# Fused attention and feed-forward kernel: copies of the turned output from another queue, and a second matmul in four 32-column tiles in chosen sessions

## The chip, the cores and the metric

The kernel runs on one core of a Trainium2 chip. The metric is the device time of one execution in microseconds; lower is better. A core has five engines that run side by side: PE (TensorE: matmuls, with weight loads listed apart as PEld), DVE (VectorE), ACT (ScalarE), POOL (GpSimd) and SP (SyncE, which here only issues transfers). Each engine executes its own instructions in the order in which they stand.

## The reference, cut to what matters

Two layers in a row. The first is attention through 32 inducing points: `h = mab(I, x)`, then `mab(x, h)`, for B = 4 batches of N = 12480 tokens with C = 128 channels. The second is a feed-forward layer with a leaky activation on each of the 49920 tokens.

```python
def mab(q, kv):                      # scale = 1/sqrt(128)
    s = scale * (q @ kv.transpose(0, 2, 1))
    s = s - s.max(-1, keepdims=True)
    a = np.exp(s)
    a /= a.sum(-1, keepdims=True) + 1e-09
    return a @ kv
h = mab(I, x)                        # I: (4, 32, 128), x: (4, 12480, 128)
y = mab(x, h)                        # (4, 12480, 128)
u = y @ w_in                         # w_in: (128, 2048)
g = np.maximum(u, 0.0) + alpha * np.minimum(u, 0.0)
out = g @ w_out                      # w_out: (2048, 128), float32
```

## The kernel before, in words

A batch is cut into six "supers" of 2048 tokens and a rest of 192. A super has four groups of 512 tokens, so a batch has NG = 25 groups (24 full ones and the rest), numbered g. The hidden width 2048 is cut into 16 blocks of 128: four row bands r times four steps j. The main loop goes over sessions (b, g, j), four to a group, two to the rest group.

What a session does, in the order of the code (lines 829 to 836):

- `fill` (line 433): four matmuls `ring<-rep,hW`, one per band r. Each contracts only 32 rows (the 32 attention weights, replicated into four partition bands in `rep`) with `hW = h @ w_in`, and writes 128 hidden units x 512 tokens to a bank of PSUM. Six banks form a ring. Then four ReLUs `gt<-ring`, some on ACT (line 457) and some on DVE (line 459); which go where is written out ahead of time by `make_plan` (line 756), a beam search over assumed costs in ns. In `make_plan` every task has a cost tuple (PE ns, engine, engine ns).
- the tasks set for the session (`at(slot, fn, j, cost)`, line 708, slot = 25 b + g). For the current batch: `b_scores` (attention scores of the next super; 128 rows contracted, four outputs of 32 partitions each), `b_rep`, `b_den`. For the next batch: `a_load` (x by a GpSimd transfer, line 131), `a_xpose` (transfer that transposes x into `xT`, issued by SP, line 145), `a_scores` (`ring<-xT,IT`, 32-partition outputs), `a_accum` (pooling, `ring<-xn,e1T`, 16 matmuls with 32-partition outputs), `h_weights` (the next batch's hW) and some small ones.
- `move(2)` (line 833): takes two entries from the list `moves`, see below.
- `mm2` of the session before (line 463): four matmuls `acc<-gt,W`, with the 128 x 128 block of the scaled `w_out` as weights and 512 tokens streaming, adding up to `acc` in PSUM, output channels on the partitions.

The output of a group therefore stands turned (channels by tokens). When a group is complete, `finish` (called by `flush` in the next session's `fill`) calls `turn` (line 537): DVE transposes 32 x 32 squares into `yT` (line 541), and after the fourth group of a super 16 `shuffle` transfers and one `leave` are put on `moves`. A shuffle (line 550) copies 32 partitions x 2 KB of `yT` to another band of 32 partitions in `yq`, SBUF to SBUF, 64 KB. `leave` (line 554) has POOL multiply by the reciprocal denominators (four instructions, line 559) and issue the 1 MB store (line 569). `yT`, `yq` and `obw` have two buffers each. The last super of the last batch and the rest groups are not turned: there `gt` is the weight operand, and `ob` (two buffers) is stored directly (lines 526 and 535).

`pin` keeps every engine's instructions, transfers included, in program order: a transfer that waits holds up what stands behind it on the same queue. The transfers of SP land in one hardware queue (q1 in the profile), those of GpSimd in a software queue (q0); the 16 DMA engines serve both.

Of the kernel before, what the change touches and what calls it, by code (L numbers as in the profile page):

```python
# [24 lines left out]
def kernel(  # L25
# [30 lines left out]
    def pin(bi):  # L56
        ins = bi.ins
        e = ins.engine
        if e in last:
            tc.add_manual_dep(  # L60
                ins,
                last[e],
                mybir.DependencyInfo(
                    mybir.DependencyClass.NoSync, mybir.DependencyReason.DATA
                ),
                reason="program order",
            )
        last[e] = ins.name
        return bi
# [26 lines left out]
    def mm(o, lhsT, rhs, start=True, stop=True, **kw):  # L96
        return pin(nc.tensor.matmul(o, lhsT, rhs, start=start, stop=stop, **kw))  # L97
# [160 lines left out]
    def a_scores(st, u):  # L258
        ps = bank()
        if u < NS:  # L260
            for q in range(NQ):
                mm(ps[32 * q : 32 * q + 32, :], IT[:], st.xT[:, u, q, :])
            e1 = work.tile([P, GRP], bf16, name="e1", tag="e1")
            pin(nc.scalar.activation(  # L264
                out=e1[:], in_=ps[:], func=EXP, scale=scale, accum_out=st.es[:, u : u + 1]
            ))
            e1T = work.tile([P, NB, P], bf16, name="e1T", tag="e1T")
            pin(nc.sync.dma_start_transpose(out=e1T[:], in_=e1[:]))
        else:
            mm(ps[0:M, :REM], IT[:], st.xTr[:].rearrange("c j p -> c (j p)"))  # L270
            pin(nc.scalar.activation(
                out=e1r[:, :, :PR],
                in_=ps[0:M, :REM].rearrange("m (j p) -> m j p", j=JR),
                func=EXP, scale=scale, accum_out=st.es[0:M, u : u + 1],
            ))
            e1T = work.tile([P, JR, M], bf16, name="e1Tr", tag="e1Tr")
            pin(nc.sync.dma_start_transpose(
                out=e1T[:], in_=e1r[:].rearrange("m j p -> m (j p)")
            ))
        st.e1T[u] = e1T  # L280
# [69 lines left out]
    def b_scores(st, s):  # L350
        ps = bank()
        if s < NS:
            for q in range(NQ):
                mm(ps[32 * q : 32 * q + 32, :], st.hT, st.xT[:, s, q, :])
            e2 = work.tile([P, GRP], bf16, name="e2", tag="e2")
            pin(nc.scalar.activation(out=e2[:], in_=ps[:], func=EXP, scale=scale_of(st)))  # L356
            w = GRP
        else:
            mm(ps[0:M, :REM], st.hT, st.xTr[:].rearrange("c j p -> c (j p)"))
            e2 = work.tile([M, REM], bf16, name="e2r", tag="e2r")  # L360
            pin(nc.scalar.activation(out=e2[:], in_=ps[0:M, :REM], func=EXP, scale=scale_of(st, M)))
            w = REM

        nq = NQ if s < NS else 1
        st.d[s] = dram.tile([32 * nq, w], bf16, name="e2d", tag="e2d" if s < NS else "e2dr")
        pin(nc.sync.dma_start(out=st.d[s][:], in_=e2[:]))
        st.e2[s] = e2
# [45 lines left out]
    def turned(b, g):  # L413
        return g < NS * NQ and (b, g // NQ) != (B - 1, NS - 1)
# [10 lines left out]
    def move(n):  # L425
        for _ in range(min(n, len(moves))):
            moves.pop(0)()
# [32 lines left out]
        flush()  # L460
        return gt

    def mm2(st, g, j, gt):
        pp, nb, cp = shape_of(g)
        acc = acc_of(st.b, g)
        begun = (g % 2 == 1 and st.b + g > 1) or cp > 1
        for r in range(4):
            if turned(st.b, g):
                mm(
                    flat(acc), W1[:, r * NJ + j, :], gt[:, r, :],  # L470
                    start=(j == 0 and r == 0 and not begun),
                    stop=False, skip_group_check=True,
                )
                continue
            for i in range(cp):
                c = r * NJ + j * cp + i
                for k in range(nb):
                    k0 = (i * nb + k) * pp
                    mm(
                        acc[:pp, k, :], gt[:, r, k0 : k0 + pp], W1[:, c, :],  # L480
                        start=(j == 0 and r == 0 and i == 0 and k == 0 and not begun),
                        stop=False, skip_group_check=True,
                    )
        if j == NJ // cp - 1 and st.b * NG + g > 0:
            held.append((st, g))
# [51 lines left out]
    def turn(st, s, q, acc):  # L537
        if q == 0:
            st.yT[s] = wide_pool.tile([P, 4, NQ, NB, 32], f32, name="yT", tag="yT")
        yT = st.yT[s]  # L540
        pin(nc.vector.transpose(  # L541
            out=yT[:, :, q, :, :].rearrange("p a j c -> p j a c"),
            in_=acc[:].rearrange("p j (a c) -> p j a c", a=4),
        ))
        if q < NQ - 1:
            return
        yq = wide_pool.tile([P, 4, NQ, NB, 32], f32, name="yq", tag="yq")

        def shuffle(a, k):
            pin(nc.sync.dma_start(  # L550
                out=yq[32 * a : 32 * a + 32, k], in_=yT[32 * k : 32 * k + 32, a]
            ))

        def leave():
            rd = st.rden[s]
            ob = wide_pool.tile([P, NQ, NB, C], f32, name="obw", tag="obw")
            for q in range(NQ):
                rq = rd[:, :, q : q + 1]
                pin(nc.gpsimd.tensor_tensor(  # L559
                    out=ob[:, q].rearrange("p j (k c) -> p j k c", k=4),  # L560
                    in0=yq[:, :, q].rearrange("p k j c -> p j k c"),
                    in1=bass.AP(
                        tensor=rq.tensor, offset=rq.offset,
                        ap=[rq.ap[0], rq.ap[1], [0, 4], [0, 32]],
                    ),
                    op=MULT,
                ))
            t0 = st.b * N + s * SUP
            pin(nc.gpsimd.dma_start(  # L569
                out=out[t0 : t0 + SUP, :].rearrange("(p q) c -> p (q c)", p=P),  # L570
                in_=ob[:].rearrange("p q j c -> p (q j c)"),
            ))

        for a in range(4):
            for k in range(4):
                moves.append(lambda a=a, k=k: shuffle(a, k))
        moves.append(leave)
# [125 lines left out]
             for j in range(NJ // shape_of(g)[2])]  # L703
    states = {0: st}
    tasks = {}


    def at(slot, fn, j=1, cost=None):
        tasks.setdefault((slot, j), []).append((fn, cost))

    def late_finish():
        linear(st, [0])
# [9 lines left out]
    for b in range(B):  # L722
        base = b * NG
        for s in range(1, NS + 1):
            g = base + s * NQ - 4
            at(g, lambda b=b, s=s: b_scores(states[b], s), 3, (320, "A", 490))
            at(g + 1, lambda b=b, s=s: b_rep(states[b], s), 3)
            at(g + 2, lambda b=b, s=s: b_den(states[b], s), 3, (130, "D", 250))
        if b + 1 < B:
            n = b + 1  # L730

            def begin(n=n):
                states[n] = new_batch(n)

            at(base, begin)
            for i, u in enumerate(order):
                k = base + i * (NG - 13) // NS
                at(k, lambda n=n, u=u: a_load(states[n], u))
                at(k + 3, lambda n=n, u=u: a_xpose(states[n], u))
                at(k + 5, lambda n=n, u=u: a_scores(states[n], u), 0, (320, "A", 680))  # L740
                at(k + 8, lambda n=n, u=u: a_accum(states[n], u), 3, (240, "D", 220))
            k = base + NG - 5
            at(k, lambda n=n: h_sum(states[n]))
            at(k, lambda n=n: h_den(states[n]), 3, (250, "D", 500))
            at(k + 1, lambda n=n: h_transpose(states[n]), 1, (300, "D", 250))
            at(k + 1, lambda n=n: h_weights(states[n]), 3, (320, "D", 600))
            at(k + 2, lambda n=n: b_scores(states[n], 0), 1, (320, "A", 490))
            at(k + 2, lambda n=n: h_linear(states[n]), 3, (80, "D", 250))
            at(k + 3, lambda n=n: b_rep(states[n], 0), 0)
            at(k + 3, lambda n=n: b_den(states[n], 0), 1, (130, "D", 250))  # L750
# [78 lines left out]
    for b, g, j in fills:  # L829
        gt = fill(states[b], g, j)  # L830
        for fn, _ in tasks.pop((b * NG + g, j), []):
            fn()
        move(2)
        if prev is not None:
            mm2(*prev)
        prev = (states[b], g, j, gt)
    mm2(*prev)
    move(len(moves))
# [32 lines left out]
```

The softmax here doesn't subtract the row's maximum and nothing guards it: scores larger than these inputs give would overflow.

## Time and profile before

| | before |
|---|---|
| median of 8 runs (lowest to highest) | 603.64 us (599.92 to 617.72) |
| the profiled execution, its own time | 603.91 us |
| its span on the core | 602.1 us |
| PE busy | 573.7 us (95%), 4518 matmuls |
| DVE busy | 517.9 us (86%) |
| ACT busy | 502.3 us (83%) |
| POOL busy | 143.7 us (24%) |
| main loop, first to last matmul | from 24.9 us to 593.4 us |
| mean granted clock of PE | 0.984 |

Busy times overlap, so they do not add up to the span. The page names shapes as weights (rows * columns), then what streams: "128\*32 128x512" is a matmul that contracts 128 rows into 32 outputs while 512 columns stream. In the timeline the first column is the start in microseconds, the second the length of the merged stretch; in brackets stand the idle time before it and what ended it. [...]the distance between starts, not the length, is what it costs in a row of others.

### The profile page before, as it was taken

To read this page: it belongs to the slowest core of one execution; us is meant where nothing else is said; L and a number is where in the kernel's file an instruction comes from. 1 tells how busy PE (TensorE), PEld (TensorE's weight loads), DVE (VectorE), ACT (ScalarE), POOL (GpSimd) and SP (SyncE) were. 2 spreads that over 40 slices of the span, in tenths; PEclk is the share of its full clock that TensorE was granted. 3 is DMA by queue.
4 is the path that set the end of the run, shared out by engine and by line. 5 is a ranking of instruction groups with operands and counts; after the bars stand their busy time and mean duration, and the time that the engine had idled before them with its cause. 6 is when DMAs were issued, how large, how long until landed. Compare 5 with 4: busy or idle time off the path is not lost.

```text
span 602.1 us, 12844 instructions
## 1 busy us (share of the span) xinstructions
PE 573.7 (95%) x4518; PEld 209.6 (35%) x4518; DVE 517.9 (86%) x869; ACT 502.3 (83%) x987; POOL 143.7 (24%) x196
## 2 busy tenths in 40 slices
PE   5899997999999998999999999799999999999994
PEld 4533332333343332333333333233334333333373
DVE  3588996889989997998988899698998999999983
ACT  2579886888889986888889999689888999999983
POOL 6620123032034030302330403203113303203303
PEclk9899998999999999999999999899999999999998
DMA  9794587973558859777346978797445443353343
GB/s 198 180 191 80 127 187 154 206 205 84 153 161 205 176 152 194 174 162 205 119 120 158 210 171 187 150 210 186 106 144 158 147 105 111 85 175 123 106 141 117
DMA packets 95216, 93.66 MB, mean 156 GB/s; under 512 B 60224, under 2 KB 75856, under 8 KB 92208
## 3 DMA queue, kind: packets, MB, share of 16 engines
q1 hardware_dynamic: 86288, 53.03, 39.1%
q0 software_dynamic: 8720, 39.29, 24.2%
q8 instruction: 35, 0.57, 0.4%
q10 hardware_dynamic: 144, 0.52, 0.2%
q14 instruction: 29, 0.24, 0.1%
HBM read 40.20 MB, written 28.75 MB: 115 GB/s over the span
## 4 chain that ended last, share of the span: by engine, by line
PE 81%; DMA 9%; SPq 4%; issue 2%; ACT 2%; DVE 1%; POOL 1%; POOLq 0%; DVEq 0%; ACTq 0%
PE acc L97 56%; PE ring L97 23%; DMA xT<-xn 6%; SPq L550 2%; ACT gt L457 2%; PE ring L174 1%; SPq L374 1%; DMA winT<-w_in_b 1%; DMA ind_f<-in_inducing_dram 1%; DMA out_dram<-ob 1%; POOL obw L559 1%; SPq L145 1%; DMA rep<-e2d 0%; DVE xT L180 0%; DMA e2d<-e 0%
## 5 line engine op out<-in xcount | busy, mean ns | idle before, releaser
L457 ACT ACTIVATE gt<-ring 128x512 bf16<-128x512 f32 x899 | 469.7, 599 | 67.2 <-PE ring L97 32.6
L459 DVE TENSOR_SCALAR gt<-ring 128x512 bf16<-128x512 f32 x669 | 434.0, 685 | 58.1 <-PE ring L97 51.0
L97 PE MATMUL acc<-gt,W 128*128 128x512 bf16 x1472 | 385.8, 385 | 0.3 <-DVE yT L541 0.3
L559 POOL TENSOR_TENSOR obw<-yq,rd 128x512 f32<-128x512 f32 x92 | 93.3, 1038 | 406.4 <-DMA yq<-yT 284.4
L97 PEld LDWEIGHTS <-W 128*128 128x128 bf16 x1472 | 115.4, 98 | 165.9 <-issue 78.0
L97 PE MATMUL ring<-rep,hW 32*128 32x512 bf16 (+1 forms) x1600 | 159.5, 382 | 0.7 <-DVE hW L250 0.2
L97 PEld LDWEIGHTS <-hW 32*128 32x128 bf16 x1600 | 41.4, 91 | 162.9 <-issue 158.6
L541 DVE STREAM_TRANSPOSE yT<-acc 128x512 f32<-128x512 f32 x92 | 65.0, 706 | 1.9 <-PE acc L97 1.9
L97 PE MATMUL acc<-W,gt 128*128 128x128 bf16 (+1 forms) x384 | 25.6, 220 | 0.0
L97 PEld LDWEIGHTS <-gt 128*128 128x128 bf16 (+1 forms) x384 | 21.9, 106 | 4.2 <-issue 3.8
L97 PE MATMUL acc<-rep,hA 32*128 32x512 bf16 x92 | 17.6, 374 | 0.0
L264 ACT ACTIVATE e<-ring 128x512 bf16<-128x512 f32 x18 | 10.9, 604 | 6.7 <-PE ring L97 6.7
L97 PE MATMUL ring<-xT,IT 128*32 128x512 bf16 x72 | 7.2, 389 | 9.5 <-DMA xT<-xn 9.5
L131 POOL DMA_DIRECT2D xn<-in_x_dram x28 | 15.4, 555 | 2.4 <-DMA xn<-in_x_dram 1.6
L569 POOL DMA_DIRECT2D out_dram<-obw x23 | 13.7, 596 | 6.8 <-POOL obw L559 6.8
L199 ACT ACTIVATE e1t<-ring 128x256 bf16<-128x256 f32 (+1 forms) x13 | 4.8, 371 | 10.8 <-PE ring L97 10.6
L180 DVE COPY xT<-ring 128x1024 bf16<-128x1024 bf16 (+1 forms) x12 | 8.0, 670 | 5.2 <-PE ring L174 4.8
L356 ACT ACTIVATE e<-ring 128x512 bf16<-128x512 f32 x18 | 11.0, 612 | 0.0
L97 PE MATMUL ring<-xT,hT 128*32 128x512 bf16 (+1 forms) x98 | 10.6, 391 | 0.0
L535 POOL DMA_DIRECT2D out_dram<-ob x7 | 3.8, 537 | 27.2 <-DVE ob L526 27.0
L174 PE MATMUL ring<-ident,xn 128*128 128x128 bf16 x96 | 8.8, 249 | 0.9 <-DVE xn L672 0.9
L97 PEld LDWEIGHTS <-hT 128*32 128x32 bf16 (+1 forms) x122 | 3.7, 93 | 11.9 <-issue 11.8
(91 smaller groups left out, 135.2 us busy)
## 6 DMA issues: line engine op xcount, KB each, us to landing
yq<-yT SPq DMA_DIRECT2D x368, 64.0 KB, 2.3
out_dram<-obw POOLq DMA_DIRECT2D x23, 1024.0 KB, 4.9
rep<-e2d SPq DMA_DIRECT2D x92, 128.0 KB, 2.8
xn<-in_x_dram POOLq DMA_DIRECT2D x18, 512.0 KB, 8.8
e2d<-e SPq DMA_DIRECT2D x24, 128.0 KB, 3.9
xn<-in_x_dram POOLq DMA_DIRECT2D x10, 256.0 KB, 8.6
w_out_f<-in_moe_w_out_dram POOLq DMA_DIRECT2D x4, 256.0 KB, 11.1
out_dram<-ob POOLq DMA_DIRECT2D x4, 256.0 KB, 3.8
```

Of the source, the lines that this page charges most:

```text
L97: return pin(nc.tensor.matmul(o, lhsT, rhs, start=start, stop=stop, **kw))
L131: pin(nc.gpsimd.dma_start(out=xn[:, i * w : (i + 1) * w, :], in_=src[:, i * w : (i + 1) * w, :]))
L174: pin(nc.tensor.transpose(tp[:, k * P : (k + 1) * P], xn[:, q, j * C : (j + 1) * C], ident[:]))
L180: pin(nc.vector.tensor_copy(out=dst, in_=tp[:, :w]))
L264: pin(nc.scalar.activation(out=e1[:], in_=ps[:], func=EXP, scale=scale, accum_out=st.es[:, u : u + 1]))
L356: pin(nc.scalar.activation(out=e2[:], in_=ps[:], func=EXP, scale=scale_of(st)))
L457: pin(nc.scalar.activation(out=gt[:, r, :w], in_=ps[:, :w], func=RELU))
L459: pin(nc.vector.tensor_relu(gt[:, r, :w], ps[:, :w]))
L541: pin(nc.vector.transpose(out=yT[:, :, q, :, :].rearrange("p a j c -> p j a c"), in_=acc[:].rearrange("p j (a c) -> p j a c", a=4),))
L550: pin(nc.sync.dma_start(out=yq[32 * a : 32 * a + 32, k], in_=yT[32 * k : 32 * k + 32, a]))
L559: pin(nc.gpsimd.tensor_tensor(out=ob[:, q].rearrange("p j (k c) -> p j k c", k=4), in0=yq[:, :, q].rearrange("p k j c -> p j k c"), in1=ba ...
L569: pin(nc.gpsimd.dma_start(out=out[t0 : t0 + SUP, :].rearrange("(p q) c -> p (q c)", p=P), in_=ob[:].rearrange("p q j c -> p (q j c)"),))
```

## The change

It has four parts. `mm2` gets a flag `narrow`: with it, each 128 x 128 weight block is used as four blocks of 32 columns, each with its own matmul over the same 512 streaming tokens and its own 32 output partitions. The flag is set for a session with a score task (`b_scores`, `a_scores`), a pooling task (`a_accum`) or `h_weights`. The shuffles are issued by GpSimd instead of SP. In the last super of the last batch four entries of `moves` are taken per session instead of two. And the PE costs that `make_plan` assumes for the flagged tasks are lower (320 becomes 215, 240 becomes 200).

```diff
-    def mm2(st, g, j, gt):
+    def mm2(st, g, j, gt, narrow=False):
         pp, nb, cp = shape_of(g)
         acc = acc_of(st.b, g)
         begun = (g % 2 == 1 and st.b + g > 1) or cp > 1
         for r in range(4):
+            if turned(st.b, g) and narrow:
+                for i in range(4):
+                    sl = slice(32 * i, 32 * i + 32)
+                    mm(
+                        flat(acc)[sl, :], W1[:, r * NJ + j, sl], gt[:, r, :],
+                        start=(j == 0 and r == 0 and not begun),
+                        stop=False, skip_group_check=True,
+                    )
+                continue
             if turned(st.b, g):
                 mm(
                     flat(acc), W1[:, r * NJ + j, :], gt[:, r, :],
...
         def shuffle(a, k):
-            pin(nc.sync.dma_start(
+            pin(nc.gpsimd.dma_start(
                 out=yq[32 * a : 32 * a + 32, k], in_=yT[32 * k : 32 * k + 32, a]
             ))
...
+    narrows = set()
...
-    def at(slot, fn, j=1, cost=None):
+    def at(slot, fn, j=1, cost=None, narrow=False):
         tasks.setdefault((slot, j), []).append((fn, cost))
+        if narrow:
+            narrows.add((slot, j))
...
-            at(g, lambda b=b, s=s: b_scores(states[b], s), 3, (320, "A", 490))
+            at(g, lambda b=b, s=s: b_scores(states[b], s), 3, (215, "A", 490), narrow=True)
...
-                at(k + 5, lambda n=n, u=u: a_scores(states[n], u), 0, (320, "A", 680))
-                at(k + 8, lambda n=n, u=u: a_accum(states[n], u), 3, (240, "D", 220))
+                at(k + 5, lambda n=n, u=u: a_scores(states[n], u), 0, (215, "A", 680), narrow=True)
+                at(k + 8, lambda n=n, u=u: a_accum(states[n], u), 3, (200, "D", 220), narrow=True)
...
-            at(k + 1, lambda n=n: h_weights(states[n]), 3, (320, "D", 600))
-            at(k + 2, lambda n=n: b_scores(states[n], 0), 1, (320, "A", 490))
+            at(k + 1, lambda n=n: h_weights(states[n]), 3, (215, "D", 600), narrow=True)
+            at(k + 2, lambda n=n: b_scores(states[n], 0), 1, (215, "A", 490), narrow=True)
...
-        move(2)
+        move(4 if b == B - 1 and g >= (NS - 1) * NQ else 2)
         if prev is not None:
-            mm2(*prev)
+            mm2(*prev, narrow=(b * NG + g, j) in narrows)
```

## The prediction

> **What bounds the kernel now.** I read the page first (busy shares, clock, DMA issues), then the timeline of PE through ordinary sessions, then every place where PE departs from that rhythm, with the timelines of SP and POOL beside it, then the tail. First PE in a plain stretch and in two sessions with tasks (start, length).
>
> ```profile
> PE 573.7 (95%) x4518; PEld 209.6 (35%) x4518; DVE 517.9 (86%) x869; ACT 502.3 (83%) x987; POOL 143.7 (24%) x196
> 200.14 0.40 PE L97 MATMUL ring<-rep,hW 32*128 32x512 bf16 x4
> 200.46 0.40 PE L97 MATMUL ring<-xT,IT 128*32 128x512 bf16 x4
> 200.79 1.04 PE L97 MATMUL acc<-gt,W 128*128 128x512 bf16 x4
> 201.76 0.40 PE L97 MATMUL ring<-rep,hW 32*128 32x512 bf16 x4
> ...
> 221.09 0.40 PE L97 MATMUL ring<-xT,hT 128*32 128x512 bf16 x4
> 221.32 0.40 PE L97 MATMUL ring<-xn,e1T 128*32 128x128 bf16 x16
> 221.65 1.04 PE L97 MATMUL acc<-gt,W 128*128 128x512 bf16 x4
> ```
>
> There are no gaps: PE sets the pace, 1.62 us for the score session (200.14 to 201.76) and 1.30 for a plain one. The starts also give the price of a change of tile shape. Scores followed by pooling, both with 32-column tiles, take 0.23 (221.09 to 221.32); scores followed by full-width mm2 take 0.33 (200.46 to 200.79), and fill to mm2 0.33. A change of shape costs 0.10 us.
>
> Now the largest break in that rhythm, with the transfers around it and DMA shares by stretch (the last three columns are granted clock, DMA share, GB/s).
>
> ```profile
> 73.42 4.06 POOL L559 TENSOR_TENSOR obw<-yq,rd 128x512 f32<-128x512 f32 x4 [39.24 <-DVE gt L459]
> 77.78 0.60 POOL L569 DMA_DIRECT2D out_dram<-obw  x1 [0.30 <-POOL obw L559]
> 78.38 1.07 POOL L131 DMA_DIRECT2D xn<-in_x_dram  x2
> ...
> 79.20 2.33 SPq L550 DMA_DIRECT2D yq<-yT  x2
> 84.35 6.63 SPq L145 DMA_TRANSPOSE xT<-xn  x1
> ...
> 90.06 0.40 PE L97 MATMUL ring<-rep,hW 32*128 32x512 bf16 x4
> 93.64 0.40 PE L97 MATMUL ring<-xT,IT 128*32 128x512 bf16 x4 [3.19 <-DMA xT<-xn]
> 99.02 0.40 PE L97 MATMUL ring<-rep,hW 32*128 32x512 bf16 x4
> ...
> 84.00:88.00 4.00, 4.00 (x25) 1.23 (x24) 3.93 (x7) 3.59 (x8) 0.00 (x0) 1.00 1.08 220
> 96.00:100.00 4.00, 4.00 (x19) 1.13 (x18) 2.78 (x5) 2.90 (x7) 0.09 (x1) 0.73 0.58 141
> ```
>
> PE waits 3.19 us for a transposed x, and the granted clock then falls (0.73 in 96 to 100). From 90.06 to 99.02 lie three sessions, worth 1.62 + 1.30 + 1.30 = 4.22; they took 8.96, so 4.74 is lost. The same place in the next two batches: three sessions from the fill at 233.98 to that at 242.22 lose 4.02, three from 377.49 to 386.44 lose 4.73. That is 13.5 in all. The cause: POOL had stood 39 us in its first `leave`, then issued a 1 MB store and two loads of x at once. The transposition of SP stands behind shuffles and meets DMA engines that are full (share 1.08), so it lands after 9.25 us where others take 4.3.
>
> Last, the tail.
>
> ```profile
> 588.28 4.06 POOL L559 TENSOR_TENSOR obw<-yq,rd 128x512 f32<-128x512 f32 x4 [5.50 <-issue]
> 593.38 1.07 POOL L535 DMA_DIRECT2D out_dram<-ob  x2 [0.16 <-issue]
> 598.01 0.42 DVE L526 TENSOR_TENSOR ob<-acc,rdr 96x256 f32<-96x256 f32 x1 [5.76 <-DMA out_dram<-ob]
> ```
>
> PE is done at 593.4; the last multiply starts at 598.0, since its buffer is held by a store that POOL could issue only behind the late `leave`.
>
> **The change part by part.**
>
> *Narrow mm2.* The order of the built program has 944 matmuls of 32 columns in place of 236, so 59 sessions are narrow. Counting changes of shape along PE's order gives 852 before and 799 after: 53 fewer, x 0.104 us = 5.5. Six sessions win nothing, since a full-width task stands between. What the narrow form itself costs: 708 more matmuls and weight loads. Here a rule speaks against the change. The Trainium skill, "TensorE: Matmul & The Clock Gate", section "Part 3: Packing small matmuls", says that weight loads overlap running matmuls only when their row groups differ; all narrow loads use all rows. By its "LDWEIGHTS" formula (columns / 1.2 ns) 16 loads of 32 columns would stand in the open, an estimate of 0.43 us per session, 25 us in all. The row of pooling answers: 16 loads and 16 matmuls of 4 x 128 columns took 0.33 with the change of shape, so 0.23 for 512 streamed columns per tile, the same as four score matmuls in one go. Those 16 loads added nothing, and they had a quarter of the streaming to hide in that narrow mm2 has. I take 0, with ends 0 and +25.
>
> *Evacuation.* ACT and DVE get the same instructions (899 and 669 ReLUs in both orders), in another split. A plain session asks of them 899 x 0.525 + 669 x 0.65 = 907 us over 392 sessions, 1.16 each of two engines, and about 0.09 for the transposes: 1.25 against PE's 1.30. A session with `a_scores` adds 0.75 on ACT: 1.25 + 0.38 = 1.63 against a shortened 1.52. Its neighbours have slack 0.05 each. Cost 0.1 in at most 18 sessions, some of it absorbed: +1.0, range 0 to 3.
>
> *Shuffles on POOL.* All 368 issues leave SP and enter POOL. The nearest rows are POOL's own issues, which show no dependence on size.
>
> ```profile
> L131 POOL DMA_DIRECT2D xn<-in_x_dram x28 | 15.4, 555 | 2.4 <-DMA xn<-in_x_dram 1.6
> L569 POOL DMA_DIRECT2D out_dram<-obw x23 | 13.7, 596 | 6.8 <-POOL obw L559 6.8
> ```
>
> At 0.555 us that is 204 us more on an engine busy 24%. Per super POOL then has 16 x 0.555 = 8.9, last landing 2.0, `leave` 4.4, store 0.6, two loads 1.1: 17.0. Supers come every 21.6 us at the closest (`yT` of the last batch complete at 506.07, 527.76). So POOL keeps up. Its order changes: the first `leave` stands behind 16 shuffles that can start when `yT` is complete (53.6), end at 62.6 and land by 65. So `leave` runs at 65 instead of 73.4, the store goes out at 69; of the loads around it one follows the shuffles at 62.6, one the store at 70, and the next comes behind the second super's shuffles at 85 (`yT` complete at 75.9). In the built order each of these loads has a shuffle batch or a `leave` between it and the next, so the pile of store plus two loads at 78 dissolves. Behind the waiting `leave` stand only loads with more than 10 us to spare. On SP the transposition at 84.35 loses its shuffles: scores at 79.0 let its small predecessor go near 80.5, it follows at 82, and at 4.4 us lands near 86.5, 3 us before PE asks. So the three breaks go: -13.5, and with them two waits of 0.5 for `xT` (260.8, 272.9) and one of 0.6 for `rep` (123.1), which I count at half, -0.8.
>
> A second rule speaks against this part: the skill's "DMA: Bandwidth & Descriptors", section "Issuing engines are not separate DMA queues", says that all issuers end on the same 16 engines and that spreading them saves only the sequencers' issue time. Taken alone, only the 0.59 us issues go from SP, the engines stay full at 84 to 92, and the breaks stay: the 14.3 drop out of the sum. Agreed for the bytes; but what the trace shows as full is a pile made by POOL's order, and the order changes. I take 14.3, range 0 to 15.1.
>
> *Four moves at the end.* The last super's `yT` is complete at 571.0; 16 issues end at 580, `leave` runs 582 to 586 and the store leaves at 586.5, 6 us earlier. The stores behind it land near 592, before the last multiply is due (593.5). Gain 598.0 - 593.6 = 4.4, less 0.5 for the multiply before it: -3.9, range 0 to -4.5. If that cover fails, the late store holds DVE, and the 4.4 stay.
>
> Sum: 602.1 - 5.5 - 13.5 - 0.8 - 3.9 + 1.0 = 579.4 of span, plus 1.8 around it (603.91 - 602.1): 581.2. The profiled execution is 0.27 above the median of 603.64, so 581 us against the median.
>
> **The rivals.**
>
> *The DMA breaks stay* (or move to another load), by the second rule: 581 + 14.3 = 595. For it: shuffles now share one in-order software queue with loads and stores, so a shuffle behind a load lands with it, 8 us later, and POOL waits. Against: the spacing above.
>
> *Evacuation binds.* ACT and DVE are at 83 and 86%; if the shape changes saved on PE turn into waits for banks, the 5.5 return: 581 + 5.5 = 586.5. For it: waits of 0.15 to 0.2 us near the `h` tasks today.
>
> *POOL becomes the bound, slower.* If one shuffle holds POOL longer than the loads do, POOL takes 16 x + 8.1 per super against 21.6; it decides from x = 0.85 us on. At 1.1 us it needs 25.7, 4 us x 23 supers = 94 too much, less the 23 of gains: near 675; at 0.95 us, 23.3, 39 too much: near 620. DVE would stand at `yT`, then ACT and PE behind full banks. Against: POOL's issues stand at 0.53 to 0.60 us in back-to-back rows; but none of them goes SBUF to SBUF over 32 partitions.
>
> *Open weight loads:* 581 + 25 = 606, slower.
>
> That the change does not do what it says is out: the built order shows the 944 narrow matmuls and POOL's 368 issues.
>
> **How the numbers follow.** The main case 0.60, breaks stay 0.14, evacuation binds 0.13, POOL bound 0.07, open loads 0.03, a mixture near the old time 0.03. A measurement of this kernel can tell about 0.5% (3 us) from no change. Faster by more: 0.60 + 0.14 + 0.13 = 0.87; within: 0.03; slower: 0.10. Low end: all breaks and waits (15.1), tail 4.5, shapes 6, no cost: 578, and 1 less for the spread of runs: 577. The high end takes in the evacuation case and most of the stay case: 595. Left out are the slower cases and the edges, 0.2.
>
> **What would show it.** Right: mm2 narrow at 0.97 us from start to fill, 0.23 instead of 0.33 before it; the xT waits and clock dips near 90, 234 and 378 gone; POOL near 345 us busy with issues of 0.56; the last multiply within 1 us of PE's end. Wrong: a shuffle issue over 0.85 us on POOL, DVE waiting before L541, weight loads opening gaps inside narrow mm2, or waits for xT at other loads.

## The result, and the profile after

| | before | after |
|---|---|---|
| median | 603.56 us (32 runs, 599.41 to 617.72) | 597.78 us (11 runs, 586.55 to 608.72) |
| profiled execution, its span | 602.1 us | 585.0 us (its time 586.80) |
| PE busy | 573.7 us | 564.9 us |
| POOL busy | 143.7 us | 324.2 us |
| mean granted clock of PE | 0.984 | 0.995 |
| sum of PE's waits for `xT` | 9.8 us | 4.6 us |

The ratio of times is 0.978 (95% interval 0.974 to 0.983). It leaves out runs more than 1.5% above the fastest of their kernel, which are many here, so the medians lie closer together (0.990) than the ratio says. The forecast was 581 us (577 to 595), faster with 0.87. The sign was right. By the ratio the change stands for 590.5 us (0.978 x 603.56), inside the range; the profiled execution lies inside it too, the median of all runs 2.8 us above it. So there are two things to explain: why the profiled execution stopped at 586.8 and not at 581, and why most executions need 5 to 22 us more than that one.

In sums and tables here, a wait for `xT` is the distance from the start of the fill before to the start of the scores, less the usual 0.33 us. That is 0.06 to 0.08 us more than the idle time in the brackets of the timeline.

The page and the costliest groups of after come first (in a group: busy us, mean ns, then idle time of the engine before it and what ended it), with two rows of the DMA issues (last number: median us from issue to landing).

```profile
PE 564.9 (97%) x5226; PEld 213.0 (36%) x5226; DVE 517.9 (89%) x869; ACT 501.2 (86%) x987; POOL 324.2 (55%) x564
L559 POOL DMA_DIRECT2D yq<-yT x368 | 180.4, 498 | 143.0 <-DVE yT L550 86.8
yq<-yT POOLq DMA_DIRECT2D x368, 64.0 KB, 3.4
xT<-xn SPq DMA_TRANSPOSE x18, 7.1
```

A shuffle holds POOL for 0.50 us, and POOL mostly waits for DVE to deliver `yT`: it is not the bound. But the last row is new: the median landing of a transposed x was 4.4 us before, and is now 7.1.

PE's timeline where scores and pooling precede a narrow `mm2`:

```profile
216.89 0.40 PE L97 MATMUL ring<-xT,hT 128*32 128x512 bf16 x4
217.11 0.40 PE L97 MATMUL ring<-xn,e1T 128*32 128x128 bf16 x16
217.34 1.04 PE L97 MATMUL acc<-gt,W 128*32 128x512 bf16 x16
218.31 0.40 PE L97 MATMUL ring<-rep,hW 32*128 32x512 bf16 x4
```

From pooling to narrow `mm2` are 0.23 us (the change of shape is gone), and the 16 narrow matmuls take 0.97 us from their start to the next fill, as four full-width ones do. Their 16 weight loads add no time that shows.

The place of the largest break of before, the scores of the same x tile, and then the next one (PE, then SP and POOL):

```profile
90.56 0.40 PE L97 MATMUL ring<-rep,hW 32*128 32x512 bf16 x4
90.88 0.40 PE L97 MATMUL ring<-xT,IT 128*32 128x512 bf16 x4
...
101.73 0.40 PE L97 MATMUL ring<-rep,hW 32*128 32x512 bf16 x4
103.49 0.40 PE L97 MATMUL ring<-xT,IT 128*32 128x512 bf16 x4 [1.36 <-DMA xT<-xn]
```
```profile
94.53 1.94 SPq L145 DMA_TRANSPOSE xT<-xn  x1
```
```profile
90.74 4.06 POOL L568 TENSOR_TENSOR obw<-yq,rd 128x512 f32<-128x512 f32 x4 [4.47 <-DMA yq<-yT]
95.10 0.59 POOL L578 DMA_DIRECT2D out_dram<-obw  x1 [0.30 <-POOL obw L568]
95.68 0.55 POOL L131 DMA_DIRECT2D xn<-in_x_dram  x1
```

Scores follow the fill after 0.32 us at 90.88: the wait of 3.19 and the clock dip after it are gone. But at 101.73 the next x tile is late: a `leave` put its store and the load behind it on the queue within 0.6 us, right beside the transposition of 94.53, which took 8.9 us to land. In this execution five such waits remain (1.04, 1.43, 1.53, 0.28 and 0.34 us), none followed by a clock dip.

Last the tail of after (POOL, SP, DVE):

```profile
577.75 0.54 POOL L544 DMA_DIRECT2D out_dram<-ob  x1 [3.77 <-DVE ob L535]
```
```profile
579.53 0.32 SPq L544 DMA_DIRECT2D out_dram<-ob  x1
```
```profile
579.09 0.42 DVE L535 TENSOR_TENSOR ob<-acc,rdr 96x256 f32<-96x256 f32 x1 [1.16 <-PE acc L97]
```

The last multiply now follows PE at once and no longer waits for a store: PE's last stretch of matmuls runs from 577.06 to 579.05, and the 1.16 us in brackets is how long DVE was idle until then. Yet the span ends at 585.0, 5.9 us after that multiply and 7.28 us after POOL's last transfer was issued; before, 4.1 us passed from the multiply to the end.

### The profile page after: what moved, and what is told of

Its sections match the earlier page's. It is cut to its first block, busy times and chain, and to the rows that moved or that the text cites. A ratio compares the mean times of both kernels' runs of the same rounds, so it can differ in the third digit from the quotient of the medians.

```text
span 585.0 us, 14237 instructions
## 1 busy us (share of the span) xinstructions
PE 564.9 (97%) x5226; PEld 213.0 (36%) x5226; DVE 517.9 (89%) x869; ACT 501.2 (86%) x987; POOL 324.2 (55%) x564
## 4 chain that ended last, share of the span: by engine, by line
PE 64%; DMA 23%; POOL 6%; issue 3%; ACT 2%; SPq 1%; DVE 0%; POOLq 0%; ACTq 0%; DVEq 0%
PE acc L97 45%; PE ring L97 19%; DMA xn<-in_x_dram 8%; DMA yq<-yT 8%; DMA xT<-xn 6%; POOL obw L568 3%; POOL yq L559 2%; ACT gt L457 1%; DMA winT<-w_in_b 1%; POOL out_dram L578 0%; SPq L374 0%; POOL xn L131 0%; DMA e2d<-e 0%; SPq L666 0%; DVE gt L459 0%
## 5 line engine op out<-in xcount | busy, mean ns | idle before, releaser
L97 PE MATMUL acc<-gt,W 128*128 128x512 bf16 (+1 forms) x2180 | 383.0, 381 | 0.3 <-DVE yT L550 0.3
L559 POOL DMA_DIRECT2D yq<-yT x368 | 180.4, 498 | 143.0 <-DVE yT L550 86.8
L97 PEld LDWEIGHTS <-W 128*128 128x128 bf16 (+1 forms) x2180 | 121.7, 97 | 155.7 <-issue 67.0
L578 POOL DMA_DIRECT2D out_dram<-obw x23 | 13.5, 586 | 6.8 <-POOL obw L568 6.8
```

Of the source, the lines that this page charges most:

```text
L559: pin(nc.gpsimd.dma_start(out=yq[32 * a : 32 * a + 32, k], in_=yT[32 * k : 32 * k + 32, a]))
L578: pin(nc.gpsimd.dma_start(out=out[t0 : t0 + SUP, :].rearrange("(p q) c -> p (q c)", p=P), in_=ob[:].rearrange("p q j c -> p (q j c)"),))
```

## The experiments

All were timed in turn with the kernel before. For runs 1 to 4 its median was 603.19, for 5 to 8 602.61.

### 1. The narrow tiles without the moved shuffles

```diff
         def shuffle(a, k):
-            pin(nc.gpsimd.dma_start(
+            pin(nc.sync.dma_start(
...
-        move(4 if b == B - 1 and g >= (NS - 1) * NQ else 2)
+        move(2)
```

> The narrow second matmul and the lower planner costs alone; shuffles stay on SP, two moves per session. If the three parts add up as in the sum (theory), only the 53 changes of shape go: PE's row from scores to mm2 at 0.23 instead of 0.33, 5.5 us off, 598 us, with the three long waits for xT near 90, 234 and 378 and their clock dips still there and the last multiply still 4 to 5 us behind PE. Rival, the whole gain of the change comes from the shapes: then near 587 to 590. Rival, evacuation binds: no gain, 603.

Measured: 604.73 (602.00 to 615.89), ratio 1.004 (1.001 to 1.007); profiled span 600.2. PE at one of the old breaks (the second batch), and the transposition it waits for:

```profile
230.83 0.40 PE L97 MATMUL ring<-rep,hW 32*128 32x512 bf16 x4
235.39 0.62 PE L97 MATMUL ring<-xT,IT 128*32 128x512 bf16 x4 [4.17 <-DMA xT<-xn]
```
```profile
225.63 7.57 SPq L145 DMA_TRANSPOSE xT<-xn  x1
```

The narrow tiles alone gain nothing in the runs, and 1.9 us in the profile. PE arrives earlier at every score session, but x does not: the waits for `xT` grew from 9.8 us in the profile of before to 12.6, and the time at half clock near 234 from 3.4 us to 6.8. (The 12.6 takes in a wait of 1.2 at 273.4, which the profile puts down to ACT, but which ends as an x tile lands.) Most of what shortens PE between two deadlines that another engine sets was lost in the next wait.

### 2. The moved shuffles alone

```diff
         def shuffle(a, k):
-            pin(nc.sync.dma_start(
+            pin(nc.gpsimd.dma_start(
```

> The shuffles issued by GpSimd alone; mm2 full width, two moves per session. Theory: the three long waits shrink to waits of 0 to 1.5 us, no clock dips in the loop in the profiled execution, so 10 to 14 us off there, about 590, but with a wide spread from run to run (590 to 612) as the changed kernel has, since single waits for xT now and then pass 2 us and bring a clock dip of another 1.7 us. Rival, the spread belongs to the narrow matmuls: then this one is as tight as the kernel before (within 3 us).

Measured: 590.86 (586.47 to 604.15, four runs), ratio 0.979 (0.974 to 0.984), the same ratio as the whole change; profiled span 588.8. PE at the place of the first break, in this run:

```profile
90.70 0.40 PE L97 MATMUL ring<-rep,hW 32*128 32x512 bf16 x4
91.99 0.40 PE L97 MATMUL ring<-xT,IT 128*32 128x512 bf16 x4 [0.90 <-DMA xT<-xn]
```

A wait of 0.90 stands where 3.19 was. By these ratios the gain of the change is that of this one word. What the narrow tiles add to it can be read by comparing the profiles between the start of session 14 and that of session 390: 531.04 us here, 527.57 in after, 3.47 less, although after has 4.62 us of `xT` waits in it and this one 3.87. So they save 3.47 + 0.75 = 4.2 us where nothing else holds PE. The medians of a handful of runs each (590.86 and 597.78) do not show that, since they vary by more; run 3 shows one reason.

### 3. The change with two moves at the end

```diff
-        move(4 if b == B - 1 and g >= (NS - 1) * NQ else 2)
+        move(2)
```

> The changed kernel with two moves per session to the end. By the prediction's step the four moves bring the tail's 4 us: then the last multiply waits again for a store, 4 us slower than the changed kernel. Rival: on POOL the shuffles of the last super do not wait for the sessions, since nothing holds them but yT, so the number of moves per session changes only where leave stands among the direct stores; with two per session one more store stands ahead of leave, and the tail is as good as with four: within 1 us.

Measured: 599.42 (595.68 to 606.88, six runs), ratio 0.995 (0.991 to 1.000); profiled span 596.5. The tail is as good as after's: here too the last multiply waits 1.16 us for PE, and the span ends 7.28 us after POOL's last transfer was issued. So the fourfold moves gain nothing, and the 11.5 us between the two profiled spans must come from elsewhere. The instructions of PE (by its weight loads, since some matmul records are missing from the trace), DVE, ACT and SP are the same as in after, in the same order, and POOL's differ only in the last super. Up to there this is a second execution of the same program. PE, SP and POOL near 100 us, and a stretch row:

```profile
101.75 0.40 PE L97 MATMUL ring<-rep,hW 32*128 32x512 bf16 x4
107.52 0.62 PE L97 MATMUL ring<-xT,IT 128*32 128x512 bf16 x4 [5.37 <-DMA xT<-xn]
```
```profile
94.79 7.60 SPq L145 DMA_TRANSPOSE xT<-xn  x1
```
```profile
93.60 0.59 POOL L578 DMA_DIRECT2D out_dram<-obw  x1 [0.30 <-POOL obw L568]
94.18 0.55 POOL L131 DMA_DIRECT2D xn<-in_x_dram  x1
```
```profile
106.00:110.00 4.00, 2.48 (x24) 0.74 (x24) 0.00 (x0) 0.69 (x2) 3.75 (x8) 0.52 0.72 161
```

Compare with the rows of after. There the transposition was issued at 94.53, and the store and load followed at 95.10 and 95.68. Here store and load came at 93.60 and 94.18, and the transposition at 94.79, behind them: its landing took 12.7 us, PE waited 5.4, and the clock fell to 0.52 (the stretch row: granted clock, DMA share and GB/s are its last three numbers). The same happened at 241.30 (11.6 us, a wait of 4.2). How the 11.5 us between the two profiles come about can be followed from session to session. The waits for `xT` are 11.0 us against 4.6, so 6.4. The sessions right after the two long waits ran in part at half clock (6.8 us from 106.2 on, of which 1.3 lie in the wait itself, and 3.4 us from 253.0 on) and lost 2.5 and 1.5. A fill at 219.20, drawn out from 0.40 to 1.36 us while `rep` landed, lost another 1.2 with the session after it, and the loop began 0.15 earlier. So 10.4 of the 11.5 us are waits for x tiles and the clock that they cost.

### 4. The change with the transposition one group earlier

```diff
-                at(k + 3, lambda n=n, u=u: a_xpose(states[n], u))
+                at(k + 2, lambda n=n, u=u: a_xpose(states[n], u))
```

> The changed kernel with the transposition of x one group (four sessions, about 5.6 us) earlier, slot k + 2 instead of k + 3. Theory: what is left of the waits, and the spread from run to run, is xT landing 7 to 9 us after its issue beside shuffles where 4.3 is the time alone; 5.6 us more room takes all waits for xT away: profiled span near 580, granted clock 0.995 or more in every run, all runs within 580 to 585. Rival: the spread comes from elsewhere (rep, or the loads of x themselves, which a transposition issued earlier would only wait for): spread and median stay near 598.

Measured: 601.23 (592.06 to 610.88), ratio 0.990 (0.986 to 0.994); profiled span 607.6. The time from the issue of the transposition to PE's demand rose as meant, from 8.3 us (median of after) to 13.6, and it did not help. SP, PE and three stretches (last columns: granted clock, DMA share, GB/s):

```profile
92.11 5.97 SPq L145 DMA_TRANSPOSE xT<-xn  x1
```
```profile
105.55 0.40 PE L97 MATMUL ring<-rep,hW 32*128 32x512 bf16 x4
115.66 0.62 PE L97 MATMUL ring<-xT,IT 128*32 128x512 bf16 x4 [9.71 <-DMA xT<-xn]
```
```profile
92.00:96.00 4.00, 4.00 (x73) 1.51 (x71) 3.68 (x8) 3.17 (x7) 1.39 (x3) 1.00 1.03 198
96.00:100.00 4.00, 3.84 (x27) 1.26 (x25) 3.72 (x7) 3.93 (x9) 0.00 (x0) 1.00 1.25 78
100.00:104.00 4.00, 4.00 (x30) 1.24 (x26) 3.98 (x7) 3.59 (x8) 0.00 (x0) 1.00 1.31 47
```

One group earlier is where loads are issued (`a_load` at `k` in steps of two groups, `a_xpose` at `k + 2`), so the transposition meets a load more often. This one, with a load 0.7 us behind it and eight shuffles issued between 88.92 and 92.82, landed after 23.5 us. By the time that their packets took, the DMA engines were more than full (1.31), and they moved 47 GB/s. More lead is no cure if it leads into the traffic.

### 5. The change with half of the bytes in every shuffle

```diff
-                out=yq[32 * a : 32 * a + 32, k], in_=yT[32 * k : 32 * k + 32, a]
+                out=yq[32 * a : 32 * a + 32, k, 0:2], in_=yT[32 * k : 32 * k + 32, a, 0:2]
...
-                    in0=yq[:, :, q].rearrange("p k j c -> p j k c"),
+                    in0=yq[:, :, q % 2].rearrange("p k j c -> p j k c"),
```

> The changed kernel with each shuffle halved: the same 368 issues on GpSimd, but 32 KB instead of 64 KB; the multiplies use the first two groups of a super twice, so the output of the other two groups is not computed. Theory A (a shuffle on the other queue no longer stands ahead of the transposition but shares the 16 DMA engines with it): the landing of xT, 7.1 us median after the change, falls to about 5, the PE waits for xT (4.6 us in the profiled run) fall under 1.5, and with them go the runs that are 10 to 20 us longer: median near 584, longest run under 592. Rival B (loads of x stretch it, not shuffles): landing stays near 7 us, median 595 to 600. Rival C (the spread of runs has nothing to do with the waits, it is the clock of the chip): waits go, but runs still lie between 583 and 606.

Measured: 594.88 (592.07 to 600.21, four runs), ratio 0.989 (0.982 to 0.995). The median landing of `xT` is 5.4 us, against 7.1 in after; the theory of the shared engines asked for 5, but run 3, with whole shuffles, has 5.2, so this fall proves nothing. The time did not follow. Two waits of 4.3 and 3.6 us were left, and both have the same neighbours. The first of them, on POOL, SP and PE:

```profile
56.91 0.59 POOL L578 DMA_DIRECT2D out_dram<-obw  x1 [0.30 <-POOL obw L568]
57.50 0.54 POOL L131 DMA_DIRECT2D xn<-in_x_dram  x1
```
```profile
60.24 6.96 SPq L145 DMA_TRANSPOSE xT<-xn  x1
```
```profile
66.93 0.39 PE L97 MATMUL ring<-rep,hW 32*128 32x512 bf16 x4
71.52 0.62 PE L97 MATMUL ring<-xT,IT 128*32 128x512 bf16 x4 [4.19 <-DMA xT<-xn]
```

The two long landings of this run stand behind a store with a load behind it. With half the bytes `leave` starts earlier, and its store and load come to stand ahead of a transposition that in after was ahead of them.

### 6. The change without loads of x in the main loop

```diff
+    kept = {}
+
     def a_load(st, u, pieces=1):
+        if st.b > 0:
+            st.xn[u] = kept[u]
+            return
...
-        st.xn[u] = xn
+        st.xn[u] = kept[u] = xn
```

> The changed kernel without the loads of x in the main loop: batches 2 to 4 use the tiles of the first batch again, so their output is not that of their own x; everything else, shuffles and transpositions too, stays. Theory A (shuffles stretch the transpositions): those beside 14 to 16 shuffles still take 7 to 9 us to land, some xT waits of 1 us or more stay, median 588 to 594. Rival B (loads do): all xT land in 4.3 to 5 us, no xT wait above 0.5 us, median near 583.

Measured: 582.07 (581.41 to 582.87, four runs), ratio 0.966 (0.963 to 0.970); profiled span 580.2. The four runs lie within 1.5 us (the change: 11 runs, 22.2 us apart), and one `xT` wait above 0.1 us is left (1.31). The place that cost 1.4 us in after and 5.4 in run 3 (PE, SP, POOL):

```profile
102.07 0.40 PE L97 MATMUL ring<-rep,hW 32*128 32x512 bf16 x4
102.42 0.40 PE L97 MATMUL ring<-xT,IT 128*32 128x512 bf16 x4
```
```profile
94.30 3.64 SPq L150 DMA_TRANSPOSE xT<-xn  x1
```
```profile
94.45 0.59 POOL L583 DMA_DIRECT2D out_dram<-obw  x1 [0.30 <-POOL obw L573]
99.77 4.43 POOL L564 DMA_DIRECT2D yq<-yT  x9 [4.73 <-DVE yT L555]
```

The store stands alone, and PE does not wait. The rival was right about the time, and the theory about the landing: it is still 6.2 us in the median and up to 9.1 (at 59.58, with shuffles and neither a store nor a load near it). PE's demand comes 8.2 us after the issue (median), so a landing of 6 to 8 us is just hidden, and the load on top is what pushes it over.

### 7. and 8. Spread loads, in the kernel before and in the changed one

```diff
-            at(base, begin)
+            at(max(0, base - 13), begin)
             for i, u in enumerate(order):
                 k = base + i * (NG - 13) // NS
-                at(k, lambda n=n, u=u: a_load(states[n], u))
+                kl = max((0, 0, 1, 2)[i] if i < 4 else 0, base + 4 * i - 12)
+                at(kl, lambda n=n, u=u: a_load(states[n], u))
```

> The kernel before (shuffles on SP, full-width second matmul) with the loads of x spread: one per super from 12 groups ahead instead of one per two groups, so that in the first supers five loads stand ahead of the first waiting leave. Theory A (the three breaks of 4 to 4.7 us came from the pile of a store and two loads behind that leave, thus from POOL's order, and not from the queue on which the shuffles stand): the waits near 90, 234 and 378 go, 603 becomes 590 to 593 with the old shuffles. Rival B (the transposition is late because it stands behind shuffles on SP's queue): the waits stay, 600 to 604. A third outcome: the breaks move to another transposition, 597 to 601.

> The changed kernel with the same spread loads. Theory A (what is left is DMA traffic beside the transpositions, 9 parts shuffles and stores to 4 parts loads in the busy half of a batch; half of the loads leave it): xT waits fall from 4.6 us to 1 to 3, fewer clock dips, median 584 to 592 instead of 598. Rival B (shuffles alone set the landing, loads don't matter): median 595 to 600, xT landing near 7 us as before the spread. If the first three loads at the start of a batch now delay the first transposition: a wait of 3 us or more near 60 us, slower than 598.

Measured: 602.20 (598.34 to 613.07), ratio 0.999 (0.995 to 1.002), for the kernel before; 595.19 (587.03 to 606.69, four runs), ratio 0.980 (0.973 to 0.988), for the changed one. In the former the break near 90 is gone, but it came back one tile later (and again at 260.0, with 2.94 us). POOL and PE:

```profile
97.71 4.06 POOL L559 TENSOR_TENSOR obw<-yq,rd 128x512 f32<-128x512 f32 x4 [19.05 <-DMA yq<-yT]
102.07 0.60 POOL L569 DMA_DIRECT2D out_dram<-obw  x1 [0.30 <-POOL obw L559]
102.67 1.07 POOL L131 DMA_DIRECT2D xn<-in_x_dram  x2
```
```profile
113.08 0.40 PE L97 MATMUL ring<-rep,hW 32*128 32x512 bf16 x4
116.83 0.62 PE L97 MATMUL ring<-xT,IT 128*32 128x512 bf16 x4 [3.35 <-DMA xT<-xn]
```

POOL stands 19 us in its next `leave`, and once more a store and two loads leave together. Fewer loads in the busy half do not help as long as one stands right behind a `leave`. In the changed kernel it is the same: at 246.2 a transposition followed its store by 4.3 us and its load by 3.8, landed after 14.1 us and cost 6.3.

### What the eight runs say together

For the kernels with shuffles on GpSimd and the transposition at its old slot, these are the places where a store and a load were both issued between 5 us before and 1.5 us after a transposition, and three with a store alone. Times of issue are relative to the issue of the transposition. The small rest tile of each batch, which has some 18 us or more to spare, is left out.

| kernel, transposition at | store | load | landing of `xT` | PE waits |
|---|---|---|---|---|
| run 3, 94.79 | -1.2 | -0.6 | 12.7 | 5.4 |
| run 3, 241.30 | -1.5 | -0.9 | 11.6 | 4.2 |
| half shuffles, 60.24 | -3.3 | -2.7 | 11.2 | 4.3 |
| half shuffles, 237.34 | -1.5 | -0.9 | 11.1 | 3.6 |
| spread loads, 246.21 | -4.3 | -3.8 | 14.1 | 6.3 |
| after, 94.53 | +0.6 | +1.2 | 8.9 | 1.4 |
| shuffles alone, 94.39 | +0.5 | +1.1 | 9.7 | 0.8 |
| shuffles alone, 234.97 | +0.9 | +1.5 | 5.3 | 0 |
| spread loads, 94.95 | +0.7 | +1.2 | 8.6 | 0.5 |
| no loads, 94.30 | +0.2 | none | 8.0 | 0 |
| no loads, 118.18 | -1.1 | none | 6.1 | 0 |
| no loads, 232.56 | -1.0 | none | 6.3 | 0 |

With the pair ahead of the transposition, landing takes 11 us or more and PE waits at least 3.6; with the pair behind it, or with the store alone, at most 9.7 and 1.4. The window of 5 us was chosen with these rows in view: where the pair is farther ahead the effect is smaller (after, 383.43: store 6.5 us ahead, landing 8.2, wait 0.3). At 94 us, 1.8 us in the order of two queues (run 3 against after) decided over 4.0 us of waiting, and over a clock dip that came with it. When POOL reaches its store depends on when the last shuffle landed; when SP reaches the transposition depends on ACT and on the scores before it. No wait in these traces ties the two, so the race can fall differently from execution to execution, as it did in after and run 3.

## Why the prediction was right or wrong, point by point

*The sum for the profiled execution.* By its own steps, predicted and found (us of span):

| step | predicted | found |
|---|---|---|
| narrow `mm2`, less evacuation | -5.5 + 1.0 | -4.2 |
| the three breaks | -13.5 | -13.2 |
| other waits for transfers | -0.8 | +3.7 |
| tail | -3.9 | -2.8 |
| start (first fill at 24.32 instead of 24.87) | 0 | -0.6 |
| sum | -22.7 | -17.1 |

Found is read so: narrow from the stretch between sessions 14 and 390 (run 2); other waits from the `xT` waits (9.8 us before, of which 8.9 are the breaks and 0.9 the rest; 4.6 after); the tail from the start of session 390 to the end (11.13 before, 8.37 after); the breaks are what is left of the 13.78 us that the loop gained from its first fill to session 390, so their 13.2 is a remainder and not a measurement of its own.

*Narrow `mm2`: right, and it needed the other part.* The 0.10 us per change of shape and the hidden weight loads came as worked out; of the two answers weighed, the row of pooling was right. The rule that weight loads overlap matmuls only when their row groups differ (the Trainium skill, "TensorE: Matmul & The Clock Gate", section "Part 3: Packing small matmuls"), an estimate of +25 us, does not hold in this trace: 16 loads with all rows and 16 matmuls took 0.97 us, as four full-width ones do. What the prediction did not see is that its terms do not add freely: by themselves the narrow tiles gain nothing (run 1), because most of what they save comes back in the waits and the clock dip behind them.

*The three breaks: right in the profile, by a mechanism that was half right.* They go when the shuffles leave SP (run 2). But the pile was not dissolved, as the step said; it shrank from a store and two loads to a store and one load. The step asked whether two loads still stand together and found a shuffle batch or a `leave` between any two; it did not ask what a `leave` itself issues, a store of 1 MB, nor what stands right behind it. And the transposition does not land "at 4.4": with the shuffles beside it and not ahead of it on one queue, it lands after 7.9 at that place (82.37), where 8.5 were to spare. By the move the room from issue to demand grew from 6.2 to 8.3 us (medians), and landing grew from 4.4 to 7.1: both by about the same (in run 3, the same program up to the last super, to 5.2). What was gained at the three breaks is that the pair no longer meets the transposition there, in this execution.

*"Behind the waiting `leave` stand only loads with more than 10 us to spare": the step that failed.* It is true of the loads' own deadlines, and beside the point: what a load costs is not its own lateness but that of the transposition which shares the engines with it. Without the loads, time is 582.07 in four runs that agree within 1.5 us. So the 15.7 us between that and 597.78 hang on the loads; the kernel before ran at 602.61 beside the one and at 603.56 beside the other. (That 582.07 is within 1.1 us of the forecast is in part chance: this kernel has less traffic than the one that was forecast.) In run 3 the trace follows the chain from a store and a load ahead of the transposition to wait and clock dip, and it makes up 10.4 of 11.5 us. That the other long executions of the changed kernel have the same cause is argued, not shown, for they have no trace. Their granted clock fits (0.977 to 0.991 where the time is 592 to 609, 0.995 and 0.999 at 587), but a low clock is no proof: the kernel before has long executions too (613.91 us at 0.973 in the series of runs 1 to 4), whose cause no trace shows, and some of those of the changed kernel may be of that kind.

*The second rule weighed*, that issuers share 16 engines whatever queue they use (the Trainium skill, "DMA: Bandwidth & Descriptors", section "Issuing engines are not separate DMA queues"): the prediction granted it "for the bytes" and took 0 from it. These traces agree with it: a transposition on SP's queue landed after 9.1 us beside shuffles on POOL's (run 6, 59.58) and after 12.7 us behind a store and a load there (run 3, 94.79), where 4.4 us is the median of before. It was worth 3.7 + 0.8 us in the profiled execution and, if the long executions have the cause that run 3 shows, some 11 more in the usual one. The rival built on it, *the breaks stay or move to another load*, with 595, was the nearest to the median (597.78), and run 3, with its two breaks at other tiles, is what it described. It had 0.14.

*POOL.* An issue from SBUF to SBUF took 0.50 us, not 0.555, and POOL was busy 324 us, not 345; the bound at 0.85 was far. The first `leave` ran at 68.2 and its store left at 72.5 (predicted 65 and 69), since the shuffles landed later.

*The tail.* The multiply came right behind PE, as predicted, and counted from session 390 it came 4.6 us earlier, but 1.8 us are given back: the program ends 7.28 us after POOL's last transfer was issued, in after and in runs 2 and 3 alike. The prediction took the last multiply for the end of the chain. And the four moves are not what does it: with two the stretch from session 390 to the end is 8.37 us, as with four, in run 3 and also in run 2, where the last multiply still waited 2.58 us for a store. The move of the queue brought it.

*Range.* It held the profiled execution and the 590.5 us of the ratio. That is more the width of the range, drawn to take in the rivals, than the main case: 590.5 is 9.5 us above 581, and that a race between POOL and SP decides over clock dips was not among the cases. It did not hold the median, because a spread of runs of 1 us was put into it, though the 8 runs of the kernel before that were known lay between 599.92 and 617.72.

What was not tried: loads in the half of a batch in which nothing is transposed, or an order that forces POOL's store and load behind the transposition. By the run without loads either would have up to 15 us to win (an estimate, 597.78 - 582.07), if the loads do no harm in their new place. Whether the narrow tiles improve the median on top of the moved shuffles stays open too: the traces say 4.2 us, the spread of the runs hides it.

## What to carry to other kernels

Before costing a transfer at nothing because it has time to spare, ask which transfer with a close deadline it will meet on the DMA engines, and look above all for what stands right behind an instruction that waits: it will all leave at once. Moving transfers to a second queue took away the order between them, not the traffic; in the profile of after the room gained on one side was paid back in landing time. And where two engines' queues race for the same DMA engines, one profile is one outcome: take a second one before believing the first.

## What the runs showed of the hardware that was not expected

- The transposition of an x tile, which lands after 4.2 to 4.4 us where it is least disturbed, often took 7 to 9 us beside shuffles, 11 to 14 behind a store and a load (13.7 to 16.8 in run 4), and 23.5 once, when the engines, by their records busier than full (1.31), moved 47 GB/s.
- Of the waits of PE above 2.4 us in the loop nearly all came with 3.4 to 10 us at half clock, during the wait or right after it (the shortest, 2.41 us at 236.8 in before, with 3.4); the one of 3.5 us that ended at 248.46 in the run with half shuffles did not. No wait at or below 2.0 us did. The half clock between 24 and 32 us that most of these profiles show, at the start of the loop, follows no such wait.
- 16 narrow matmuls of 32 columns with all rows, each with its own weight load, took 0.97 us for four weight blocks, the same as four of 128 columns.
- The program ended 7.28 us after the last transfer that GpSimd issued, in after and in runs 2 to 5 and 8 (5.7 in the run without loads), although SP's later and last store needed only 1.7 us to land. What takes these 7.28 us, the traces do not show.
